# Loads by heads, one engine per q/k copy, MoE steps in the order of w_in, a third PSUM bank, batch 1 three slots later

## The chip, the cores and the metric

One core of one Trainium2 chip. The metric is the device time of one execution in microseconds (us); the kernel before takes 350.98 us, the median of four runs from 350.35 to 351.89. Engines are called by the profile's names: PE (TensorE matmul; PEld its weight loads), DVE (VectorE), ACT (ScalarE), POOL (GpSimd), SP (SyncE). POOL also issues the loads from HBM.

## The reference

A sliding-window attention with ALiBi bias is followed, without a return to HBM, by a two-layer feed-forward with ELU (called MoE in the code, though there is one expert). Inputs are float32; the kernel computes in float16 with float32 sums.

```
q, k, v: (8 batches, 8 heads, 576 positions, 64)
scores = q k^T / 8;  key within the last 128 positions: scores - slope_h * distance, else -1e9
attn = softmax(scores);  x = (attn v) as (4608 tokens, 512)
h = x w_in          (512 x 2048)
g = where(h > 0, h, exp(min(h, 0)) - 1)
out = g w_out       (2048 x 512)
```

## The kernel before

**Attention.** 576 positions are five key/query blocks: four of 128, stored interleaved, and a tail of 64. One step of attention is one entry of `BANKS`, a block and two or four heads, so that its scores fill one PSUM bank of 512 columns; a batch has 16 steps. A step has `scores` (PE, L355; for batch 0 the bias is added by PE too, L375, for the other batches by extra rows of q and k), an exponential on ACT (L379, 512 columns), for batches 1 to 7 a minimum with a mask, `cut`, on DVE (L387), and `values` (PE, L401). When both head halves of a block are there, `normalize` divides on DVE (L421, L422), and `turn` transposes the result into `xT`, in batches 0 and 1 by PE through a PSUM bank and a DVE copy (L435, L437), later by DMA. q and k must stand with the head dimension on partitions: for batch 0 `transposes_half`, for batch 1 `transposes`, both by PE and copied out of PSUM by `put` (L305), which gives one half of the columns to DVE and the other, after it, to ACT. From batch 2 on DVE's `squares` (L324) and DMAs do it.

**Values.** v is loaded in another layout, and 32-partition pieces of it are copied into the buffers `VP`, by DVE (L119) or by POOL (`place_by_pool`, L124, two pieces to a call). Sixteen pieces make a batch. POOL does twelve pieces of batches 0 and 1 each and all of the rest.

**MoE.** A block of 512 tokens takes 16 first-layer steps and 16 second-layer steps. A first-layer step, `hidden`, is 16 (or 8 wider) matmuls into one PSUM bank `hp` (L458), an exponential on ACT (L462) and a clamp on POOL (L463); `elu` on DVE (L470) joins the two in the next slot and frees the bank. There are two such banks, so that a step must wait for the `elu` two steps earlier. A second-layer step, `output`, is four matmuls of 512 columns into the one bank `op` (L501); each fourth is followed by an ACT copy (L505), which frees that bank, and by the stores. Matmul step m of the first layer uses the columns of w_in, and of the second the rows of w_out, in four chunks that POOL loads one by one.

**The order.** It is written out by hand. The last loop runs over slots: in each it emits `hidden`, the `elu` of the slot before, the tasks entered for the slot by `at`, and `output`. `HID` and `OUT` say which step falls into which slot, `LATER` pushes them back from some step on. Each engine executes its instructions in this order and waits where an operand isn't there. A DMA that POOL issues uses one of eight completion semaphores in turn, so that the ninth issue waits for the first one's landing. `warm` (L533) issues matmuls whose result nobody reads.

```
for m in range(16 * NTB):
    late = LATER.get(m, late)
    HID[4 + m + late[0]] = OUT[13 + m + late[1]] = divmod(m, 16)
for b in range(B):
    s0 = 16 * b                        # scores of step s in slot s0 + s
```

In the kernel before, batch 0 takes slots 0 to 15, batch 1 slots 16 to 31 and so on; the first layer starts in slot 4, the second in slot 13, and the last output step is in slot 160. A slot of the steady part (one first-layer step, one second-layer step, one attention step) is some 2.1 us long.

Of the kernel before, what the change touches and what calls it, by code (L numbers as in the profile page):

```python
# [12 lines left out]
ALU = mybir.AluOpType  # L13
# [6 lines left out]
def kernel(  # L20
# [20 lines left out]
    LATER = {16: (0, 1), 24: (1, 2), 30: (2, 2), 32: (3, 3), 40: (4, 4)}  # L41
# [9 lines left out]
    ps_x = ctx.enter_context(tc.tile_pool(name="ps_x", bufs=1, space=PSUM))  # L51
    ps_h = ctx.enter_context(tc.tile_pool(name="ps_h", bufs=2, space=PSUM))
# [34 lines left out]
    def load_half(b, w, a):  # L87
        if b not in stq:
            stq[b] = stage.tile([128, 2, H, 4, D], F16, name="stq")
        nc.gpsimd.dma_start(  # L90
            stq[b][64 * a:64 * a + 64, w, :, :, :].rearrange("p h j d -> p h (j d)"),
            (q, k)[w][b, :, 256 * a:256 * a + 256, :].rearrange("h (p j) d -> p h (j d)", j=4))
# [24 lines left out]
    def place_v4(b, n):  # L117
        for j in range(4):
            V.tensor_copy(VP[b % 2][32 * j:32 * j + 32, n, :, 0:D],  # L119
                          vs[b][32 * n:32 * n + 32, :, j, :])  # L120

    def place_by_pool(b, n, u):
        for j in (2 * u, 2 * u + 1):
            nc.gpsimd.tensor_scalar(  # L124
                out=VP[b % 2][32 * j:32 * j + 32, n, :, 0:D], in0=vs[b][32 * n:32 * n + 32, :, j, :],
                scalar1=1.0, scalar2=0.0, op0=ALU.mult, op1=ALU.add)
# [12 lines left out]
    with tc.manual_schedule():  # L139
# [3 lines left out]
        posi = one([128, 576], I32, "posi")  # L143
        nc.gpsimd.iota(row, pattern=[[0, 1]], base=0, channel_multiplier=1)
        nc.gpsimd.iota(col, pattern=[[1, 128]], base=0, channel_multiplier=0)
        load_half(0, 1, 0)
        load_half(0, 0, 0)
# [8 lines left out]
        load_v_half(0, 1)  # L156
        load_wi(2)
        load_wi(3)
# [73 lines left out]

        def terms():

            nc.gpsimd.tensor_scalar(out=is96, in0=rowf, scalar1=96.0, scalar2=None, op0=ALU.is_equal)
            nc.gpsimd.tensor_scalar(out=is97, in0=rowf, scalar1=97.0, scalar2=None, op0=ALU.is_equal)
            nc.gpsimd.tensor_scalar(out=isx, in0=is97, scalar1=-1.0, scalar2=None, op0=ALU.mult)
            nc.gpsimd.tensor_scalar(out=pm[r_, :], in0=posi[r_, :], scalar1=float(-MID), scalar2=None,
                            op0=ALU.add)
            nc.gpsimd.tensor_scalar(out=TQ[r_, 0:576], in0=pm[r_, :], scalar1=isx[r_, :], scalar2=is96[r_, :],  # L240
                            op0=ALU.mult, op1=ALU.add)
            nc.gpsimd.tensor_scalar(out=TK[r_, 0:576], in0=pm[r_, :], scalar1=is96[r_, :],
# [4 lines left out]
        def group_rows():  # L247
# [5 lines left out]
            for t in (TQ, TK):  # L253
                V.tensor_copy(t[g_, 256:512], t[g_, 0:256])

# [16 lines left out]
        zeros()  # L272
        groups()

# [6 lines left out]
        def transposes_half(a, hq):  # L281

            if a:
                t = ps_o.tile([128, 2, 2, 4, 2, 32], F16, name="tph", tag="op")
            else:
                t = ps_s.tile([128, 2, 2, 4, 2, 32], F16, name="tp", tag="sps")
            p = slice(64 * a, 64 * a + 64)
            for w in (1, 0):
                for g in range(4):
                    for j in range(2):  # L290
                        nc.tensor.transpose(
                            t[:, w, :, g, j, :],
                            stq[0][p, w, 4 * hq + g, 2 * j:2 * j + 2, :].rearrange("p a d -> p (a d)"),
                            ident[p, p])
            for n in range(2):
                put(t[:, :, n], QK[0][0:64, 2 * a + n, :, 4 * hq:4 * hq + 4, :])
# [371 lines left out]
```

## Time and profile before

| | |
|---|---|
| median of 4 runs | 350.98 us (350.35 to 351.89) |
| profiled execution, its own time | 350.35 us |
| span of its records | 348.6 us |
| PE busy | 329.1 us (94%) |
| DVE busy | 247.9 us (71%) |
| POOL busy | 222.0 us (64%) |
| ACT busy | 189.5 us (54%) |
| matmuls that nobody reads (L533) | 90, 9.6 us |
| HBM read, written | 36.70 MB, 9.44 MB |

Busy time is the union of the records of an engine; a matmul's record overlaps the next one's, so that start to start is the better measure for PE (four output matmuls show 1.03 us as one piece, and the next instruction starts 0.86 us after their start). A row of the timeline gives the start, the length, the engine, the line and operation, the tiles, and in brackets how long the engine was idle before and what ended that.

### The profile page before, as it was taken

To read this page: it belongs to the slowest core of one execution; us is meant where nothing else is said; L and a number is where in the kernel's file an instruction comes from. 1 tells how busy PE (TensorE), PEld (TensorE's weight loads), DVE (VectorE), ACT (ScalarE), POOL (GpSimd) and SP (SyncE) were. 2 spreads that over 40 slices of the span, in tenths; PEclk is the share of its full clock that TensorE was granted. 3 is DMA by queue.
4 is the path that set the end of the run, shared out by engine and by line. 5 is a ranking of instruction groups with operands and counts; after the bars stand their busy time and mean duration, and the time that the engine had idled before them with its cause. 6 is when DMAs were issued, how large, how long until landed. Compare 5 with 4: busy or idle time off the path is not lost.

```text
span 348.6 us, 9340 instructions
## 1 busy us (share of the span) xinstructions
PE 329.1 (94%) x3610; PEld 242.8 (70%) x3610; DVE 247.9 (71%) x556; ACT 189.5 (54%) x335; POOL 222.0 (64%) x344
## 2 busy tenths in 40 slices
PE   6998799877999999999999999999999999999995
PEld 5876677655676677777777777777777777666653
DVE  5664797587689789978987889789977666433330
ACT  4457675654556565555565565555555665444431
POOL 9698858999748965894688488748832223333320
PEclk9699999999999999999999999999999999999999
DMA  8999997259994599469956974895432222121122
GB/s 105 197 207 202 138 152 102 40 100 181 182 146 100 115 176 130 100 118 185 135 116 104 200 109 109 127 187 97 107 75 57 55 54 47 40 59 31 30 50 73
DMA packets 66075, 39.53 MB, mean 113 GB/s; under 512 B 31024, under 2 KB 59952, under 8 KB 65968
## 3 DMA queue, kind: packets, MB, share of 16 engines
q0 software_dynamic: 41904, 18.35, 44.7%
q1 hardware_dynamic: 23952, 20.46, 27.0%
q8 instruction: 28, 0.46, 0.5%
q10 hardware_dynamic: 176, 0.13, 0.1%
q14 instruction: 15, 0.12, 0.1%
HBM read 36.70 MB, written 9.44 MB: 132 GB/s over the span
## 4 chain that ended last, share of the span: by engine, by line
PE 69%; POOL 13%; DVE 5%; DMA 5%; issue 4%; ACT 2%; SPq 1%; POOLq 0%; ACTq 0%; DVEq 0%
PE hp L458 30%; PE op L501 28%; POOL VP L124 6%; PE sp L355 6%; PE av L401 4%; POOL e L463 3%; DMA wi<-in_moe_w_in_dram 2%; DVE g L470 2%; DMA stt<-in_q_dram 1%; DVE tt L324 1%; SPq L507 1%; DVE xn L422 1%; DVE EX L387 1%; ACT EX L379 1%; POOL stq L83 1%
## 5 line engine op out<-in xcount | busy, mean ns | idle before, releaser
L458 PE MATMUL hp<-xT,wi 128*128 128x256 f16 (+3 forms) x1536 | 150.4, 246 | 8.0 <-DVE g L470 5.2
L458 PEld LDWEIGHTS <-wi 128*128 128x128 f16 x1536 | 120.6, 98 | 49.6 <-DVE g L470 10.2
L463 POOL TENSOR_SCALAR e<-e 128x512 f32<-128x512 f32 x144 | 89.9, 624 | 100.3 <-ACT e L462 92.4
L462 ACT ACTIVATE e<-hp 128x512 f32<-128x512 f32 x144 | 86.0, 597 | 120.4 <-PE hp L458 113.6
L501 PE MATMUL op<-wo,g 128*128 128x512 f16 x560 | 143.0, 379 | 0.0
L470 DVE SCALAR_TENSOR_TENSOR g<-e,hp 128x512 f16<-128x512 f32 x144 | 96.9, 673 | 45.8 <-POOL e L463 45.4
L124 POOL TENSOR_SCALAR VP<-vs 32x512 f16<-32x512 f16 x120 | 76.4, 637 | 10.0 <-DMA vs<-in_v_dram 1.8
L379 ACT ACTIVATE EX<-sp 128x512 f16<-128x512 f32 x128 | 75.9, 593 | 11.7 <-PE sp L375 7.9
L387 DVE TENSOR_TENSOR EX<-EX,band 128x512 f16<-128x512 f16 x112 | 56.9, 508 | 27.3 <-ACT EX L379 26.5
L501 PEld LDWEIGHTS <-g 128*128 128x128 f16 x560 | 49.6, 98 | 35.0
L355 PE MATMUL sp<-QK 128*128 128x128 f16 (+3 forms) x576 | 50.1, 214 | 0.8 <-ACT QK L305 0.8
L401 PE MATMUL av<-VP,EX 128*128 128x65 f16 x576 | 38.8, 194 | 1.8 <-DVE EX L387 1.8
L401 PEld LDWEIGHTS <-EX 128*128 128x128 f16 x576 | 32.4, 98 | 5.4 <-DVE EX L387 2.8
L422 DVE TENSOR_TENSOR xn<-av,rden 128x256 f16<-128x256 f32 x80 | 34.0, 425 | 2.7
L324 DVE STREAM_TRANSPOSE tt<-stq 128x512 f16<-128x512 f16 x48 | 33.1, 697 | 0.0
L355 PEld LDWEIGHTS <-QK 128*128 128x128 f16 (+1 forms) x576 | 31.5, 97 | 2.0 <-ACT QK L305 1.2
L505 ACT COPY ob<-op 128x512 f32<-128x512 f32 x35 | 20.5, 586 | 10.3 <-PE op L501 5.2
L421 DVE RECIPROCAL rden<-av 128x4 f32<-128x4 f32 x80 | 13.9, 174 | 3.8 <-PE av L401 3.4
L533 PE MATMUL spare<-ident 128*128 128x128 f16 x90 | 9.6, 288 | 1.6 <-DVE ident L165 1.6
L305 ACT COPY QK<-tp 64x512 f16<-64x512 f16 (+1 forms) x8 | 6.3, 795 | 7.9 <-DVE QK L305 7.9
L533 PEld LDWEIGHTS <-ident 128*128 128x128 f16 x90 | 8.4, 135 | 1.8 <-DVE ident L165 1.6
L343 DVE COPY QK<-tpt 64x512 f16<-64x512 f16 x16 | 6.7, 417 | 0.3 <-PE tpt L338 0.2
(75 smaller groups left out, 134.0 us busy)
## 6 DMA issues: line engine op xcount, KB each, us to landing
out_dram<-ob SPq DMA_DIRECT2D x126, 64.0 KB, 1.9
QK<-tt SPq DMA_DIRECT2D x48, 128.0 KB, 2.3
stq<-in_k_dram POOLq DMA_DIRECT2D x7, 512.0 KB, 8.2
stq<-in_q_dram POOLq DMA_DIRECT2D x7, 512.0 KB, 8.5
vs<-in_v_dram POOLq DMA_DIRECT2D x7, 512.0 KB, 11.3
wi<-in_moe_w_in_dram POOLq DMA_DIRECT2D x4, 512.0 KB, 11.7
wo<-in_moe_w_out_dram POOLq DMA_DIRECT2D x4, 512.0 KB, 13.5
QK<-QK SPq DMA_DIRECT2D x1, 1280.0 KB, 8.6
```

The source lines that it names most:

```text
L124: nc.gpsimd.tensor_scalar(out=VP[b % 2][32 * j:32 * j + 32, n, :, 0:D], in0=vs[b][32 * n:32 * n + 32, :, j, :], scalar1=1.0, scalar2=0.0, ...
L324: V.transpose(out=tt[b][:, dh, w, hs, :, :].rearrange("p h j i -> p (h j) i"), in_=stq[b][:, w, hs, :, 32 * dh:32 * dh + 32].rearrange("p ...
L355: nc.tensor.matmul(t[:, o:o + n], qk[0:r, kc, 1, h, :], qk[0:r, qc, 0, h, 0:n], start=b > 0 or o == 0, stop=b > 0)
L379: nc.scalar.activation(e[:, 0:512], t, AF.Exp, scale=0.125)
L387: V.tensor_tensor(out=e, in0=e, in1=band[:, c:c + n].unsqueeze(1).broadcast_to([128, 512 // n, n]), op=ALU.min)
L401: nc.tensor.matmul(a[:, l, :], e[:, c:c + 128], vp[:, n, h, 0:D + 1], start=st, stop=sp)
L422: V.tensor_tensor(out=xnt[b, i][:, 4 * half:4 * half + 4, :], in0=a[:, :, 0:D], in1=r.unsqueeze(2).broadcast_to([128, 4, D]), op=ALU.mult)
L458: nc.tensor.matmul(p[:, l * w + u0:l * w + u1], w_in_sb[:, c, fc * 128:(fc + 1) * 128], xT[:, c, x0:x0 + u1 - u0], start=(c == 0), stop=(c ...
L462: nc.scalar.activation(e, p, AF.Exp)
L463: nc.gpsimd.tensor_scalar(out=e, in0=e, scalar1=1.0, scalar2=0.0, op0=ALU.min, op1=ALU.max)
L470: V.scalar_tensor_tensor(out=gs[t][:, f0:f0 + nf, c0:c0 + w], in0=sh(es.pop((t, j))), scalar=1.0, in1=sh(hps.pop((t, j))), op0=ALU.subtrac ...
L501: nc.tensor.matmul(ops[t], gs[t][:, fc, ts * 128:(ts + 1) * 128], w_out_sb[:, fc, :], start=(fc == 0), stop=(fc == NFC - 1))
```

## The change

- The first halves of k and q of batch 0 are loaded in two groups of four heads. The first group's DMAs now stand ahead of the two index generators (`iota`) from which the identity matrix is made.
- `transposes_half` treats one of q and k at a time, in a bank of its own; ACT copies k, DVE copies q, in four pieces of 256 columns each. The banks come from other pools than before.
- `place_v` replaces `place_v4` and `place_by_pool` and takes the engine. In batch 0's first two blocks ACT, DVE and POOL share the pieces; in batches 1 and 2 POOL and ACT take one piece each where POOL took two.
- The terms of the bias rows are made on DVE, in slots 3 to 10, where POOL made most of them in slot 0. Loads of w_in (chunks 2, 3), of w_out and of the second half of v are issued by POOL between its pieces, in slots 0 to 10.
- The first eight first-layer steps come in the order 0, 1, 4, 5, 2, 6, 3, 7 (those that use chunks 0 and 1 of w_in before those that use 2 and 3), and from step 2 on two slots later. The bank for the transposes of `turn` is given up (they use those of the scores), and `hp` gets it as its third.
- Batch 0's steps 6 to 15 come 2 slots later, all other batches 5 slots later; first-layer steps from 16 on move by 5 slots in all, second-layer steps by 3. The last output step is in slot 163. There are 68 unread matmuls instead of 90.

```diff
-    LATER = {16: (0, 1), 24: (1, 2), 30: (2, 2), 32: (3, 3), 40: (4, 4)}
+    LATER = {16: (3, 4), 24: (4, 5), 30: (5, 5), 32: (6, 6), 40: (7, 7)}
-    ps_x = ctx.enter_context(tc.tile_pool(name="ps_x", bufs=1, space=PSUM))
-    ps_h = ctx.enter_context(tc.tile_pool(name="ps_h", bufs=2, space=PSUM))
+    ps_h = ctx.enter_context(tc.tile_pool(name="ps_h", bufs=3, space=PSUM))
...
+    def place_v(b, n, js, engine):
+        for j in js:
+            o, i = VP[b % 2][32 * j:32 * j + 32, n, :, 0:D], vs[b][32 * n:32 * n + 32, :, j, :]
+            if engine is nc.gpsimd:
+                engine.tensor_scalar(out=o, in0=i, scalar1=1.0, scalar2=0.0, op0=ALU.mult, op1=ALU.add)
+            elif engine is V:
+                engine.tensor_copy(o, i)
+            else:
+                engine.copy(o, i)
...
+        load_half(0, 1, 0, 0, 4)
+        load_half(0, 0, 0, 0, 4)
         nc.gpsimd.iota(row, pattern=[[0, 1]], base=0, channel_multiplier=1)
         nc.gpsimd.iota(col, pattern=[[1, 128]], base=0, channel_multiplier=0)
-        load_half(0, 1, 0)
-        load_half(0, 0, 0)
+        load_half(0, 1, 0, 4, 8)
+        load_half(0, 0, 0, 4, 8)
...
-        def transposes_half(a, hq):
+        def transposes_half(a, hq, w, pool, tag):
...
             for n in range(2):
-                put(t[:, :, n], QK[0][0:64, 2 * a + n, :, 4 * hq:4 * hq + 4, :])
+                for odd in range(2):
+                    (nc.scalar.copy if w else V.tensor_copy)(
+                        QK[0][0:64, 2 * a + n, w, 4 * hq:4 * hq + 4, :].rearrange(
+                            "p h (a o i) -> p h a o i", o=2, i=32)[:, :, :, odd, :],
+                        t[64 * odd:64 * odd + 64, n])
...
+        first = [0, 1, 4, 5, 2, 6, 3, 7]
         for m in range(16 * NTB):
             late = LATER.get(m, late)
-            HID[4 + m + late[0]] = OUT[13 + m + late[1]] = divmod(m, 16)
-        warm(34)
-        transposes_half(0, 0)
+            t, j = divmod(m, 16)
+            HID[m + (4 if m < 2 else 6) + late[0]] = t, first[m] if m < 8 else j
+            OUT[13 + m + late[1]] = t, j
+        warm(20)
+        transposes_half(0, 0, 1, ps_h, "hp")
         warm(8)
+        transposes_half(0, 0, 0, ps_h, "hp")
+        transposes_half(0, 1, 1, ps_v, "av")
         at(0, scores, 0, 0)
-        at(0, transposes_half, 0, 1)
-        at(0, warm, 12)
-        at(0, place_v4, 0, 0)
+        at(0, transposes_half, 0, 1, 0, ps_v, "av")
+        at(0, warm, 8)
+        at(0, place_v, 0, 0, (0, 1), V)
+        at(0, place_v, 0, 0, (2,), nc.scalar)
+        at(0, place_v, 0, 0, (3,), nc.gpsimd)
+        at(0, place_v, 0, 1, (0, 1, 2), nc.gpsimd)
+        at(0, load_v_half, 0, 1)
+        at(0, load_wi, 2)
...
         for b in range(B):
-            s0 = 16 * b
+            s0 = 16 * b + (5 if b else 2)
...
+                sv = s if b == 0 and s < 6 else s0 + s
...
-                    at((13, 14, 15, 15)[hp], transposes, 1, hp)
+                    at((18, 19, 20, 20)[hp], transposes, 1, hp)
                 for n in range(8 if b else 0):
-                    at(s0 + (2 + n if b > 1 else 6 + n // 2), squares, b + 1, n)
+                    at(s0 + (2 + n if b > 1 else 4 + n), squares, b + 1, n)
...
+        at(8, terms)
+        at(3, zeros)
+        at(8, last_blocks)
+        at(5, groups)
+        at(10, group_rows)
+        at(20, place_v, 1, 0, (0, 1, 2, 3), V)
         for n in range(4):
             for u in range(2):
                 if n:
-                    at(13 + 2 * n + u, place_by_pool, 1, n, u)
-                at(21 + 2 * n + u, place_by_pool, 2, n, u)
+                    at(18 + 2 * n + u, place_v, 1, n, (2 * u,), nc.gpsimd)
+                    at(18 + 2 * n + u, place_v, 1, n, (2 * u + 1,), nc.scalar)
+                at(26 + 2 * n + u, place_v, 2, n, (2 * u,), nc.gpsimd)
+                at(26 + 2 * n + u, place_v, 2, n, (2 * u + 1,), nc.scalar)
```

## The prediction

> **What bounds the kernel now.** I read the busy shares first, then the waits of PE, then stretches of the span.
>
> ```profile
> PE 329.1 (94%) x3610; PEld 242.8 (70%) x3610; DVE 247.9 (71%) x556; ACT 189.5 (54%) x335; POOL 222.0 (64%) x344
> ```
>
> PE is the bound, and its work hardly changes. What can move is its idle time, 19.5 of 348.6 us, and the unread matmuls. The table of stretches (length; busy us and count for PE, PEld, DVE, ACT, POOL; granted clock; DMA) says where it idles:
>
> ```profile
> 1.60:6.10 4.50, 4.41 (x42) 3.99 (x42) 2.56 (x13) 2.13 (x9) 4.50 (x8) 1.00 0.89 114
> 6.10:9.50 3.40, 1.68 (x24) 1.28 (x25) 2.22 (x11) 0.93 (x2) 3.40 (x6) 1.00 1.24 159
> 9.50:16.40 6.90, 6.61 (x69) 5.84 (x69) 4.71 (x13) 2.60 (x5) 4.21 (x8) 0.51 1.33 199
> ...
> 18.70:51.20 32.50, 28.36 (x435) 23.42 (x433) 22.42 (x54) 22.02 (x34) 26.53 (x39) 1.00 1.23 173
> 51.20:57.80 6.60, 6.60 (x93) 5.22 (x92) 5.56 (x16) 4.87 (x9) 4.45 (x7) 1.00 0.74 89
> 57.80:90.70 32.90, 26.93 (x350) 19.26 (x349) 21.95 (x48) 18.08 (x30) 29.98 (x44) 1.00 0.66 112
> 90.70:200.00 109.30, 108.24 (x1219) 79.45 (x1219) 92.62 (x206) 62.35 (x114) 77.87 (x120) 1.00 0.94 139
> ```
>
> After 90.7 us PE idles 1 us in 109; nothing is to be won there. It idles 4.1 us in 18.7 to 51.2 (slots 4 to 15) and 6.0 us in 57.8 to 90.7 (slots 19 to 30), where POOL is busy 91% of the time. Note the third row: after a stretch in which PE was busy 1.68 of 3.4 us the granted clock was half for 6.9 us. The timelines of PE and POOL inside the last idle stretch show the mechanism:
>
> ```profile
> 75.12 1.55 POOL L124 TENSOR_SCALAR VP<-vs 32x512 f16<-32x512 f16 x2
> 76.76 0.61 POOL L463 TENSOR_SCALAR e<-e 128x512 f32<-128x512 f32 x1
> 77.32 0.72 POOL L104 DMA_DIRECT2D stt<-in_k_dram  x1
> 78.10 1.57 POOL L124 TENSOR_SCALAR VP<-vs 32x512 f16<-32x512 f16 x2
> ...
> 78.15 1.05 PE L458 MATMUL hp<-xT,wi 128*128 128x128 f16 x16 [0.73 <-DVE g L470]
> ```
>
> The clamp (L463) stands behind two v pieces and a load in POOL's queue, `elu` waits for it, and with two banks the first layer waits for `elu`.
>
> **The change, stretch by stretch.** I walk through the new order with the durations of these records and the waits that the order implies. Sums are against the profiled execution (span 348.6, own time 350.35); the median of the runs is 0.63 above that, and I add differences to the median.
>
> *Start to the first first-layer matmul (18.69 before).* The identity waits for two load issues more (first k load 0.87 and first q load 0.69 for eight heads; taken as 0.6 each for four), so `warm` begins at 2.97, not 1.62. Twenty unread matmuls at the first ones' 112 ns end at 5.2, where the landed k is transposed (5.48 before; earlier landing alone would be hidden behind the identity). Separate engines then copy q and k at once: four pieces of 0.29 on DVE (a 256-column DVE copy of PSUM shows 0.29) beside four of 0.37 on ACT (256 columns: 0.37), 1.5 us instead of 0.42 + 0.58 + 0.42 + 0.58 in turn. First score at 8.5 (8.73), second at 11.1 (12.12), then the slots with 16 unread matmuls less: first MoE matmul at 17.0. **-1.7.** Bounds: 0 (the later identity eats it) and -2.7 (all 22 dropped matmuls at 122 ns).
>
> *Slots 4 to 20, before 4 to 15.* PE's share of a slot, start to start: first-layer step 0.89, score and value with batch 0's bias 0.8, output step 0.86, eight transposes 0.44. Slots 6 and 7 hold no first-layer step: values, 32 transposes and a turn, 1.7 us of work, but 3.6 us long, since scores, exponential, copies and normalisation follow each other (0.65 + 0.35 + 0.75 + 0.15 idle). Slots 8 and 10 pile on DVE: bias terms (two of about 0.5, a row that DVE doesn't have; a 256-column one takes 0.34, POOL's 1.02; bounds 0.35 and 1.0) and the last blocks' mask, 3.3 together, then the group rows, 1.9. DVE's sum over slots 8 to 13 is 11.4 against PE's 11.1, begins 1.0 behind, and delays `elu`: PE waits 0.95, 0.5 and 0.4, though the third bank shifts each wait one slot back. POOL has 10.1 us here and w_in, w_out land in time (chunk 2 issued near 13.5, needed near 28). Length 38.3 against 32.5, with three first-layer steps and five output steps more done (3 x 0.89 + 5 x 0.86 = 7.0): **-1.2.** Bounds -3 and +1.5 (DVE pieces 20% longer beside POOL, as one v piece's 0.74 beside a 0.28 minimum shows is possible).
>
> *Slots 20 to 24, before 15 to 18.* Here the change adds a wait. In slot 20 ACT's queue is: exponential 0.6, two halves of transposed q/k (a pair shows 1.92, DVE's 0.68 ahead of it), a v piece, then the copy that frees `op`. A v piece on ACT has no row; 128 columns from SBUF take 0.29 beginning to end (0.21 in sequence), 1024 take 1.04, so 512 lie between 0.3 and 1.04, by interpolation 0.61. Already late from slot 18 (bias rows 1.04), the copy starts 4.8 and ends 5.4 us into slot 20, whereas the next output step is ready at 3.7. PE waits 1.7 us, and behind that wait stand the exponential of batch 1's first scores and its cut, so that the values wait 0.85 more, then 0.45. Slots 22 to 24 have no first-layer step to fill in, as the next needs batch 1's first block. Slots 21 to 23 take 7.6 us with one first-layer step; before, slots 16 to 18 took 6.66 with three: 7.6 + 2 x 0.89 - 6.66 = **+2.7.** Bounds 0 (v piece at 0.3, and the copy just in time) and +3.2.
>
> *Slots 24 to 35, before 19 to 30.* POOL's sum falls from 27 to 18 us, one v piece a slot having gone to ACT. But slots 29 to 32 have no output step (before: only slot 29), while DVE has elu 0.69, cut 0.45, a square 0.70 and half a normalisation in each of slots 25 to 32: 19.9 us in slots 25 to 33 against 16.2 of PE. The bound goes from POOL to DVE: PE waits for the cut 0.7, 1.35, 0.85, 1.8 in slots 30 to 33. By the walk 28.1 us, before 32.9 with one first-layer step and three output steps more (3.5): **-1.25.** Bounds -5 (DVE's lag bridged) and +1.
>
> *Rest:* the same slots, shifted; two output steps fewer trail at the end, but the sum of PE's work is the same: 0. Sum -1.45.
>
> *The clock.* The wait in slots 21 and 22 leaves PE 0.86 us of work in some 3.4 us, less than the 1.68 of 3.4 after which the clock was half for 6.9 us. [...] Then 6.9 us at half clock cost 3.4 us of PE work, of which 0.7 fall into waits that slots 22 to 25 have anyway: +2.7. I go by the row. Sum **+1.25**, 350.98 + 1.25 = 352.2.
>
> **The rivals.** (1) *As walked, full clock:* 349.5. [...] (2) *Not slower: TensorE runs ahead of DVE.* The third bank lets the first layer go on while the cuts are late, and slots 24 to 35 shrink to PE's own 22.6 us plus what DVE can't bridge, -5 instead of -1.25; with it, 352.2 - 3.75 = 348.5, and 345.8 at full clock. It decides once PE's idle time in these slots is under 3 us where I have 5.2. For it: from 98 to 108 us before, DVE ended up to 2.4 us behind PE's slot without stopping PE. Against: that was with values two slots after scores; batch 1 has one. (3) *Worse on both counts:* slots 6 and 7 (1.7 of 3.6 us busy) also bring half a clock, +1.9 after DVE's waits there, and DVE is stretched by ACT's and POOL's copies, +1.5: 355.6. (4) *Loads by heads do nothing:* the first score waits for the identity and copies, the start gains 0: 353.9, part of (3)'s side.
>
> **How the numbers follow.** The main case has 0.35 (own range 351 to 353.8), (1) 0.23, (2) 0.2, (3) and (4) 0.22. A measurement of this kernel can tell about 0.3%, 1.05 us, from no change. Below 349.93 lie (2) and most of (1): 0.38. Within 1.05 us lie the edges of (1) and of the main case: 0.12. Above: 0.5. The range leaves a tenth on each side: low 345.8, case (2) at full clock; high 357, (3) with the start's bound of +1.7 nearly whole.
>
> **What the profile would show.** Start: first L458 record near 17 us. Slot 20: an idle PE ahead of an output matmul near 59 us, ended by the ACT copy of `op`, about 1.7 us, and half the granted clock after it. Then PE waits for the DVE cut, 1 us and more each, near 75 to 85 us, with POOL under 80% busy. It would be wrong if ACT reaches the `op` copy in time, if PE's idle time between 18 and 95 us is below 8 us in all, or if the clock is full there.

## The result and the profile after

The changed kernel takes 349.28 us (median of 43 runs, 347.22 to 352.61), the kernel before 350.74 (64 runs): ratio 0.9957, 95% interval 0.9944 to 0.9969; the ratios here leave out slow runs, over 1.5% above the fastest of their kernel (the 352.61 is one). It is faster by 0.4%, 1.5 us; I had forecast 1.25 us slower. The profiled execution took 348.65 us (before: 350.35), with a span of 346.9 us.

The busy shares of the changed kernel, first. Its `elu` is on L468, the first layer on L456, the scores on L353, the copy of the output bank on L503.

```profile
PE 329.2 (95%) x3588; PEld 244.3 (70%) x3588; DVE 248.8 (72%) x568; ACT 200.8 (58%) x359; POOL 211.1 (61%) x326
```

PE's sum is that of before; 11 us left POOL and 11 us came to ACT. Then the stretches that answer to those shown of before (length; busy us and count for PE, PEld, DVE, ACT, POOL; granted clock; DMA): the start, slots 4 to 20, slots 21 to 23, slots 24 to 35, one step of half clock in these, and the rest.

```profile
6.80:9.50 2.70, 2.44 (x30) 1.94 (x28) 1.38 (x5) 2.20 (x7) 1.92 (x3) 1.00 1.11 138
...
20.00:55.78 35.78, 33.64 (x473) 26.24 (x471) 29.48 (x74) 24.18 (x41) 26.83 (x40) 1.00 1.21 166
55.78:63.22 7.44, 4.91 (x49) 2.87 (x48) 5.56 (x13) 6.26 (x10) 5.08 (x8) 1.00 1.09 150
63.22:91.81 28.59, 24.62 (x321) 18.61 (x320) 21.61 (x47) 22.33 (x37) 18.75 (x29) 0.94 0.62 105
84.70:88.20 3.50, 3.50 (x27) 2.44 (x25) 1.58 (x5) 1.21 (x2) 0.78 (x2) 0.51 0.67 136
91.81:200.00 108.19, 107.41 (x1219) 80.45 (x1218) 88.81 (x203) 63.07 (x114) 78.38 (x118) 1.00 0.95 139
```

The third row is where I had put the half clock. PE is busy 4.91 of 7.44 us there, and the clock is full. Slots 24 to 35 (fourth row) lost POOL as their bound: 18.75 of 28.59 us busy, before 29.98 of 32.90. PE idles 4.0 us in them instead of 6.0; between 18 and 95 us it idles 8.6 us in all, just above the 8 us that I had named as a sign of being wrong. A half clock does occur, but in the fifth row, after DVE's late cuts. (The clock record of this profile begins at 16.45 us; the 1.00 that the first row shows is not a record. The same 128-column matmuls show 314 ns up to 16.4 us and 219 ns after it, as they do before and after 16.37 us in the kernel before, where the record has the clock at half from 9.54 to 16.37 us; so the clock was half here too.)

The wait for the output bank that I had walked through (1.7 us) is there to a tenth. The timeline of PE, slots 20 to 22:

```profile
58.73 1.02 PE L499 MATMUL op<-wo,g 128*128 128x512 f16 x4 [1.67 <-ACT ob L503]
60.26 0.30 PE L399 MATMUL av<-VP,EX 128*128 128x65 f16 x4 [0.52 <-DVE EX L385]
```

The waits of PE over the whole changed kernel hold a line that no part of the prediction speaks of, the last here:

```profile
PE av L399 <- DVE EX L385: 4.3, 8, 1.3
...
PE op L499 <- ACT ob L503: 1.7, 1, 1.7
...
PE hp L456 <- DVE g L468: 0.5, 1, 0.5
...
PE sp L353 <- DMA QK<-tt: 0.3, 1, 0.3
```

It is the first score of batch 2 (slot 37), which waits for q and k of batch 2 as `collect` copies them over SP's queue. It looks small. It became the second finding of the study.

### The profile page after: what moved, and what is told of

Its sections match the earlier page's. It is cut to its first block, busy times and chain, and to the rows that moved or that the text cites. A ratio compares the mean times of both kernels' runs of the same rounds, so it can differ in the third digit from the quotient of the medians.

```text
span 346.9 us, 9316 instructions
## 1 busy us (share of the span) xinstructions
PE 329.2 (95%) x3588; PEld 244.3 (70%) x3588; DVE 248.8 (72%) x568; ACT 200.8 (58%) x359; POOL 211.1 (61%) x326
## 4 chain that ended last, share of the span: by engine, by line
PE 67%; DVE 5%; DMA 3%; ACT 2%; SPq 1%; issue 1%; DVEq 0%; ACTq 0%
PE op L499 29%; PE hp L456 29%; PE sp L353 6%; PE av L399 4%; DMA QK<-tt 2%; DVE g L468 2%; DVE tt L322 1%; DVE EX L385 1%; ACT EX L377 1%; DMA xT<-xn 1%; SPq L328 1%; ACT e L460 1%; DVE xn L420 0%; PE tpt L336 0%; SPq L505 0%
## 5 line engine op out<-in xcount | busy, mean ns | idle before, releaser
L456 PE MATMUL hp<-xT,wi 128*128 128x256 f16 (+3 forms) x1536 | 151.1, 247 | 1.1 <-DMA xT<-xn 0.5
L456 PEld LDWEIGHTS <-wi 128*128 128x128 f16 x1536 | 123.0, 98 | 39.6 <-issue 2.6
L468 DVE SCALAR_TENSOR_TENSOR g<-e,hp 128x512 f16<-128x512 f32 x144 | 96.8, 672 | 38.7 <-POOL e L461 38.0
L385 DVE TENSOR_TENSOR EX<-EX,band 128x512 f16<-128x512 f16 x112 | 54.7, 488 | 30.2 <-ACT EX L377 29.8
L121 POOL TENSOR_SCALAR VP<-vs 32x512 f16<-32x512 f16 x106 | 68.4, 645 | 12.9 <-DMA vs<-in_v_dram 5.6
L353 PE MATMUL sp<-QK 128*128 128x128 f16 (+3 forms) x576 | 50.2, 215 | 0.5 <-DMA QK<-tt 0.3
L353 PEld LDWEIGHTS <-QK 128*128 128x128 f16 (+1 forms) x576 | 31.7, 98 | 1.7 <-issue 0.6
L503 ACT COPY ob<-op 128x512 f32<-128x512 f32 x35 | 20.5, 586 | 10.0 <-PE op L499 7.6
L531 PE MATMUL spare<-ident 128*128 128x128 f16 x68 | 8.2, 301 | 3.8 <-DVE kmod L169 3.8
L125 ACT COPY VP<-vs 32x512 f16<-32x512 f16 x16 | 9.8, 615 | 0.8 <-DMA vs<-in_v_dram 0.4
L531 PEld LDWEIGHTS <-ident 128*128 128x128 f16 x68 | 6.8, 141 | 4.1 <-DVE kmod L169 3.8
L373 PE MATMUL sp<-DM,cI 128*128 128x256 f16 (+1 forms) x40 | 6.9, 279 | 0.0
```

The costliest lines, as they stand in the source:

```text
L121: engine.tensor_scalar(out=o, in0=i, scalar1=1.0, scalar2=0.0, op0=ALU.mult, op1=ALU.add)
L353: nc.tensor.matmul(t[:, o:o + n], qk[0:r, kc, 1, h, :], qk[0:r, qc, 0, h, 0:n], start=b > 0 or o == 0, stop=b > 0)
L385: V.tensor_tensor(out=e, in0=e, in1=band[:, c:c + n].unsqueeze(1).broadcast_to([128, 512 // n, n]), op=ALU.min)
L456: nc.tensor.matmul(p[:, l * w + u0:l * w + u1], w_in_sb[:, c, fc * 128:(fc + 1) * 128], xT[:, c, x0:x0 + u1 - u0], start=(c == 0), stop=(c ...
L468: V.scalar_tensor_tensor(out=gs[t][:, f0:f0 + nf, c0:c0 + w], in0=sh(es.pop((t, j))), scalar=1.0, in1=sh(hps.pop((t, j))), op0=ALU.subtrac ...
```

## The experiments

My theory for the miss: the walk without the half clock was right (349.5), and the clock depends on something finer than a half-busy 3.4 us. The rivals: the third bank did more than I gave it; the start gained more; or what was lost and won before 95 us didn't reach the end. All times are medians; each ratio is to runs of the kernel before on the same chip (350.5 to 350.7 us), with its 95% interval. The changed kernel's own ratio is 0.9957.

### The pieces on ACT, and the wait in slot 20

One edit gives only the pieces of slots 20 and 21 back to POOL:

```
-  at(18 + 2 * n + u, place_v, 1, n, (2 * u + 1,), nc.scalar)
+  at(18 + 2 * n + u, place_v, 1, n, (2 * u + 1,), nc.gpsimd if n == 1 else nc.scalar)
```

> The changed kernel, with the two v pieces of slots 20 and 21 given back from ACT to POOL. If the wait for the output bank in slot 20 (1.7 us in the changed kernel) comes from the v piece and what stands with it in ACT's queue: the piece is 0.62 us of the 1.7, so about 1.1 us of wait is left and the waits behind it shrink too, 348.3 us. If that wait only hides a later one (the values of slot 21, which wait for the cut): no change, 349.3. If POOL is late instead (values of batch 1 wait for v): 350 or more.

Measured: 348.35 us, ratio 0.9918 (0.9896 to 0.9940). The wait for the bank fell from 1.67 to 1.02 us, by the 0.6 of one piece, and the time by what was expected. (By the limit estimated below from a count of columns, the shorter wait also leaves no position of the clock's steps that would bring a half clock there: no stretch of one step's length in this profile's slots 20 to 24 holds fewer than 3,440 columns.)

A second gives all pieces of batches 1 and 2 back:

```
-  at(18 + 2 * n + u, place_v, 1, n, (2 * u + 1,), nc.scalar)
+  at(18 + 2 * n + u, place_v, 1, n, (2 * u + 1,), nc.gpsimd)
-  at(26 + 2 * n + u, place_v, 2, n, (2 * u + 1,), nc.scalar)
+  at(26 + 2 * n + u, place_v, 2, n, (2 * u + 1,), nc.gpsimd)
```

> The changed kernel, with all v pieces of batches 1 and 2 on POOL, none on ACT, as in the kernel before (13 pieces of some 0.75 us more on POOL in slots 20 to 33). Theory of my walk: POOL's sum there rises from 18 to about 28 us and the clamp stands behind the pieces again, so what the change won in slots 24 to 35 (1.25 us) is lost, and about 0.7 is won back in slot 20, where the output bank waits for ACT: 349.8. Rival: the third bank bridges POOL's queue by itself, and the move to ACT only costs the wait in slot 20: 348.3.

Measured: 350.03 us, ratio 0.9971 (0.9947 to 0.9994). By the ratios that is 0.5 us above the changed kernel, with overlapping intervals: what all the pieces on ACT are worth together is not proved by this run. But it is 1.9 us above the kernel with only two pieces given back, and these two intervals don't overlap: the pieces of slots 22 and later are worth having on ACT, those of slots 20 and 21 are not. The wait for the bank is 1.0 here too; the waits for the cut grew from 4.3 to 5.6, the longest, 2.3 us, at 85.2 us. (PE also waits 1.5 us for `elu` instead of 0.5, but at 30 to 33 us, ahead of the edit's first slot; that is not its doing.)

A third puts two more on ACT, which write again what another copy writes:

```
+  at(20, place_v, 1, 1, (3,), nc.scalar)
+  at(20, place_v, 1, 2, (1,), nc.scalar)
```

> The changed kernel with two further v pieces on ACT in slot 20 (they write again what another copy writes), so that the wait for the output bank there grows by 1.2 us, from 1.7 to 2.9. Rule that ten profiles suggest: in steps of 3.41 us, whose beginning differs from execution to execution, PE's columns are counted (those of a 64-row matmul half), and fewer than some 3,000 to 3,100 give half the clock for the next step. With the longer wait most positions of the steps have fewer (with 1.7 us a quarter of them): a half clock near 57 to 64 us in the profile, and 1.2 us for the wait plus most of 1.7 for the clock, less what is absorbed at the scores of batch 2 (0.3 to 1.3): 350.5 to 352. Rival, a step must be empty of matmuls: no half clock at 55 to 65 us, 349.5 to 350.5.

Measured: 350.18 us, ratio 0.9986 (0.9966 to 1.0005). The wait is 2.9 us, as the sum of two pieces has it, so the queue on ACT is shown as the cause of the wait. On the clock this run says nothing for the theory: the time lies in the rival's range, and in the profile the clock stayed full there, with 3,384 columns in the step around the wait (the count is explained below). By the limit estimated there 88% of the positions of the steps would have given a half clock, so either this execution was one of the few others or the limit does not hold for it; the other eleven executions have no profile.

### The third bank

The changed kernel with two banks, and the kernel before with three:

```
-    ps_h = ctx.enter_context(tc.tile_pool(name="ps_h", bufs=3, space=PSUM))
+    ps_x = ctx.enter_context(tc.tile_pool(name="ps_x", bufs=1, space=PSUM))
+    ps_h = ctx.enter_context(tc.tile_pool(name="ps_h", bufs=2, space=PSUM))
-            t = ps_s.tile([128, 4, 128], F16, name="xps", tag="sps")
+            t = ps_x.tile([128, 4, 128], F16, name="xps", tag="xps")
```

> The changed kernel with two banks for the first layer, and the bank of its own for the transposed x, as before. My walk gave the third bank only a shift of the waits in slots 8 to 13 by one slot, and left slots 24 to 35 to DVE: 0.3 to 0.9 us longer, 349.6 to 350.2. Rival 2 of the prediction (the bank lets TensorE run ahead of a late DVE and POOL): 2 to 4 us of waits of the first layer for elu come back in slots 8 to 13 and 24 to 35, 351.5 to 353.

Measured: 350.79 us, ratio 0.9998 (0.9976 to 1.0021): by the medians all of the gain is gone without the bank. PE's waits, with two banks:

```profile
PE hp L457 <- DVE g L469: 4.8, 7, 1.4
PE av L400 <- DVE EX L386: 2.9, 5, 1.3
PE op L500 <- ACT ob L504: 1.7, 1, 1.7
PE hp L457 <- DMA xT<-xn: 1.3, 1, 1.3
```

The first layer waits 4.8 us for `elu` where it waited 0.5. Part of that is taken from the wait for the cut (2.9, was 4.3). By the medians the bank is worth 1.5 us (from 0.5 to 2.4 by the intervals of the two ratios together), more than the 0.3 to 0.9 of my walk, less than rival 2 needed. Part of it lies where neither my walk nor rival 2 looked, behind slot 37: the kernel before waits once more for `elu` there, at 143.0 us, the changed kernel does not, and with two banks it waits twice, at 122.9 and 141.3 us. PE's waits between 133 and 147 us before, then between 110 and 150 us with two banks:

```profile
PE hp L458 <- DVE g L470: 0.7, 1, 0.7
```

```profile
PE hp L457 <- DVE g L469: 1.1, 2, 0.6
```

> The kernel before with the third bank alone (the transposed x goes into the scores' banks). If POOL's queue sets the pace of slots 19 to 30 (busy 91%), a bank more only shifts the waits there: 350.0 to 350.7. If the bank bridges what POOL is late by, part of the 6.0 us of idle time there goes: 347.5 to 349, and the bank would be what made the changed kernel faster.

Measured: 350.00 us, ratio 0.9986 (0.9961 to 1.0010): not told from no change. In the kernel before, the bank moves the waits from the first layer (0.3 us is left there) to the cut (4.0) and to x's transposes (1.9), which now share the scores' banks. Its profile also had a half clock from 38.3 to 45.2 us. By this run the bank alone is not shown to pay; with the rest of the change it is.

### Squares of batch 2 earlier

```
-    at(s0 + (2 + n if b > 1 else 4 + n), squares, b + 1, n)
+    at(s0 + (2 + n if b > 1 else 1 + n), squares, b + 1, n)
```

> The changed kernel, with the eight squares of batch 2 in slots 22 to 29 instead of 25 to 32. Theory: DVE is the bound in slots 29 to 33, so three squares of 0.70 us fewer there take 2 of the 3.2 us that PE waits in slots 29 to 33, and with it the half clock after them; the squares in slots 22 to 24 lie in time in which DVE waits for ACT's late queue anyway: 346.5 to 347.5. Rival: the squares delay the cuts of slots 22 to 24 by 0.7 each, what is won later is lost there: 349 to 350.

Measured: 349.78 us, ratio 0.9991 (0.9972 to 1.0011). A miss. The half clock near 85 us was absent in its profile (mean granted clock 0.998), but what was won by slot 33 came out again as waits for transfers: 1.6 us for a load of q's tail at 88.8 us, 1.1 us at the first score of batch 2, the line noticed above, and 1.1 instead of 0.5 us for the DMA-transposed x. (The 1.4 us of waits for `elu` in this profile lie at 28 to 33 us, ahead of the edit.)

### The clock: filling a wait

The changed kernel, with unread matmuls ahead of the values of slots 31 and 32:

```
+    FILL = {9: 6, 10: 20}
...
+    if b == 1 and s in FILL:
+        for _ in range(FILL[s]):
+            nc.tensor.matmul(a[:, 2 * (p % 2), :], ident, ident[:, 0:D + 1], start=True, stop=True)
```

> The changed kernel, with 26 unread matmuls of 65 columns ahead of the values of slots 31 and 32, where PE waits 0.3 and 1.3 us for DVE's cut; they write a region that the values then write anew. Theory: the half clock from 84.72 to 88.13 us comes from a stretch of 3.41 us with too few columns in it (1.41 us of PE's busy time); with 1,300 columns more in it the clock stays full, which is worth half of 3.41 us, 1.7 us, in the executions that have that stretch: 347.6 to 348.5, and no half clock near 85 us in the profile. Rival, the clock does not go by what PE does there: half clock as before, 349.3 to 349.8.

Measured: 351.26 us, ratio 1.0020 (0.9999 to 1.0040). The clock behaved as the theory said, full from 64 to 347 us. The time did not, and is some 2 us above the changed kernel's: the first score of batch 2 waited 1.3 us for its transfers instead of 0.3 and came at 95.7 us, as in the changed kernel (95.8), and the DMA-transposed x was waited for 1.9 us instead of 0.5. That second wait, which the other kernel with fillers below has too (1.8), is not explained. Nor do the executions without a profile show the fuller clock: the twelve have a mean granted clock of 0.992, as those of the changed kernel have, though a half step fewer adds 0.005. The surprise was elsewhere: this profile had a half clock at 60.68 us, in slots 21 to 23, where my prediction had put it and where the edit changes nothing.

### Where the clock's steps fall

Every change of clock in these profiles lies on a grid of 3.41 us whose beginning differs from execution to execution (6.13, 9.54 and 16.37 us in the first profile of the kernel before, 16.45, 84.72 and 88.13 in that of the changed kernel). For each step I counted the columns that PE streamed: a 512-column matmul takes 0.216 us at full clock (four begin 0.86 us before the next group), so each was spread over that rate, and a matmul with 64 rows was counted half. At this rate a step at full clock holds some 8,090 columns; the fullest on record count 8,050 to 8,100. In the 18 profiles:

```
columns in a step of 3.41 us, full clock granted   -> clock in the next step
20 steps with 1,590 to 3,127                       -> half
all others: lowest 2,977  3,076  3,076  3,087      -> full
at half clock: 2,560 2,652 2,687 2,698 2,808       -> stays half
               3,317 and more                      -> full
```

A limit near 3,050, some 38% of a full step, is my estimate from these counts; it separates both directions, with two of some 1,740 steps on its wrong side. The edges of the count are uncertain by about 100, and by more at half clock. Steps just ahead of a profile's first clock record, taken at half clock, had 3,090 and more and were followed by full clock. The half weight of 64-row matmuls is a choice of this count: counting each transpose by PE half and every other matmul whole separates the steps as well, in each direction by itself. What the clock itself goes by is not shown. By the estimated limit, a quarter of all positions of the grid give the changed kernel a half clock after slot 21, if the matmuls stand where its first profile has them. Only further executions of the unchanged kernels can test that.

> The changed kernel, unchanged, profiled once more: the profile of an execution tells where the clock's steps of 3.41 us fall in it, and that differs from execution to execution. By the rule of the column count (below some 3,050 full-row columns in a step: half clock in the next), a clock record that begins at 57.4 us or up to 0.9 us ahead of it, less whole steps, has the half clock after slots 21 and 22 that step 5 of the prediction foresaw (a quarter of executions); the others don't. The start: full clock from about 7 us in some, from about 16.4 in others, the first MoE matmul at some 15 or some 17.4 us. If the rule is wrong, the clock is as in the first profile, or changes without regard to the steps.

Measured: 347.13 us. In this execution of the changed kernel a step begins at 54.71 us. The stretches of one step each:

```profile
54.71:58.12 3.41, 1.24 (x9) 0.39 (x7) 2.40 (x6) 3.32 (x6) 1.38 (x3) 1.00 1.10 142
58.12:61.53 3.41, 3.41 (x22) 1.99 (x23) 2.03 (x6) 1.42 (x3) 3.15 (x5) 0.50 1.01 139
61.53:64.94 3.41, 3.29 (x42) 2.29 (x41) 1.46 (x3) 3.30 (x6) 1.39 (x3) 1.00 0.02 5
```

The wait fills most of the first (2,157 columns), and the next is at half clock: the clock that the prediction foresaw, in the changed kernel itself. The same wait in the first profile of the changed kernel, by its own grid, and the steps around the late cuts:

```profile
57.41:60.82 3.41, 1.58 (x13) 0.75 (x13) 2.41 (x7) 2.82 (x6) 1.44 (x3) 1.00 1.26 176
60.82:64.24 3.42, 2.50 (x22) 1.23 (x21) 2.52 (x7) 2.81 (x4) 3.17 (x5) 1.00 0.78 98
81.31:84.72 3.41, 1.40 (x22) 0.90 (x20) 3.38 (x8) 2.30 (x4) 2.73 (x5) 1.00 1.52 306
84.72:88.13 3.41, 3.41 (x25) 2.35 (x23) 1.56 (x5) 1.21 (x2) 0.76 (x2) 0.50 0.66 134
```

The wait is cut by the grid: 3,295 columns in the first step, and the clock stays full. In the third, 1,998 columns, and it is halved.

> The changed kernel, unchanged, a second such look: as for the first, and own time and clock go together: with full clock from about 7 us some 1.5 to 2.5 us shorter than with full clock from 16.4 us, and a half stretch in slots 6 and 7, 21 and 22, or 31 and 32 costing up to 1.7 us each, less what the scores of batch 2 wait for their transfers in any case.

Measured: 347.53 us; half clock at 82.57 us, after a step of 2,209 columns; full clock at slots 21 to 23 (3,544).

> The changed kernel, unchanged, a third such look: as for the first two. By the rival view (only a step without any matmul halves the clock) no execution has a half clock between 16.5 and 84 us.

Measured: 348.83 us; half clock at 23.65 us, around slots 6 and 7 (1,755 columns in the step before), and at 85.09 (2,834). No step in the three was empty of matmuls, and each has a half clock between 16.5 and 84 us (58.12, 82.57, 23.65): the rival view does not hold here.

> The kernel before, unchanged, profiled once more. By the column count its only stretches with few columns lie at the start and around 37 us (3,076 in one step of the first profile, at the edge): the half clock of the start (6.9 us in the first profile) depends on where the steps fall as well, and so does the first MoE matmul (18.69 us): between 16.5 and 19 us.

Measured: 349.84 us; half clock from 8.77 to 15.60 us, first MoE matmul at 18.67. The kernel before does the same as in its first profile.

Side by side, all from the clock records and PE's timeline (us):

```
execution          own time  full clock from  first MoE matmul  later half steps  wait of slot 37
changed, first      348.65       16.45            17.43          84.72              0.26
changed, 2nd        347.13        6.92            14.86          58.12              1.67
changed, 3rd        347.53        7.47            15.17          82.57              1.24
changed, 4th        348.83       13.41            16.28          23.65, 85.09       0.22
before, first       350.35     6.13 to 9.54, 16.37   18.69       none               none
before, 2nd         349.84     5.36 to 8.77, 15.60   18.67       none               none
```

Two things follow. In the four executions of the changed kernel the position of the grid goes with how long its start takes: the earlier the full clock, the earlier the first MoE matmul, by up to 2.6 us. And the execution with the half clock that the prediction foresaw is the fastest of the four. What that half clock cost can be read against the 3rd for a while: the sixteenth `elu` ends at 58.60 and 58.55 us, the nineteenth at 73.19 and 72.23. It cost 0.9 us by then. Behind that the pair tells nothing, since the 3rd had its own half step at 82.57 us. At slot 37 PE's lead shrinks in any case: at the twenty-fifth `elu` the four stand 2.9 us apart (90.45, 87.52, 88.11, 90.22), at the twenty-eighth 1.6 (97.96, 96.40, 96.68, 97.92), the early ones having waited longest there.

It would be wrong to conclude that half clocks cost nothing in the end. Each of the 44 executions of the changed kernel on record has its mean granted clock, from which one half step takes 0.005. The 23 with 0.992 or more have a median of 348.8 us, the 21 with 0.990 or less one of 350.0. Where their half steps fell is known for the profiled ones alone.

### Behind slot 37: a transfer that was moved

The diff moves `fill_other`, one transfer of 64 rows of 20 KB, from slot 24 to slot 30, by 6. Batch 1, with the `collect` transfers of batch 2 that share its queue (slots 24 to 31, now 29 to 36), moves by 5 slots (three more than batch 0). What changed is what stands behind it. Before, it was issued at 75.1 us, the next collect at 82.8, and it landed at 83.7. In the changed kernel it is issued at 79.8 us, the next collect 0.7 us behind it, and it lands after 8.9 us, at 88.7; that collect lands at 89.1. The collects of the changed kernel (79 to 97 us), issues and time to landing:

```profile
L328 SPq DMA_DIRECT2D QK<-tt x8: 520/636/2613, 78.5 to 89.0; - x8
...
DMA to landing us min/median/max: 2.4/9.0/10.8
```

Before, seven collects were issued after 80 us:

```profile
L330 SPq DMA_DIRECT2D QK<-tt x7: 513/540/591, 82.8 to 91.3; - x7
...
DMA to landing us min/median/max: 3.1/3.5/7.0
```

The median landing rose from 3.5 to 9.0 us. One edit puts the transfer ahead again:

```
-        at(30, fill_other)
+        at(27, fill_other)
```

> The changed kernel with the copy of batch 1's bias rows to the other q/k buffer (64 rows of 20 KB, one transfer) in slot 27 instead of 30. Theory, from four traces in which TensorE comes to the scores of batch 2 at times 3.4 us apart in slot 33 and at the same time, 95.6 to 95.8 us, in slot 37: the collected q/k of batch 2, whose transfers stand behind this copy, set the time there and absorb what is won or lost in slots 21 to 36. With the copy ahead of them the first ones land 3 us earlier; in executions with no half clock in slots 21 to 36 PE then gains 1 to 2 us, in the others 0.3: 348.3 to 349. Rival: the loads of batch 3's q and k, which start at the same time, hold the collected rows back just as long: 349.3.

Measured: 347.12 us (6 runs), ratio 0.9897 (0.9866 to 0.9929), 0.6% below the changed kernel and more than expected. The collects with it:

```profile
L328 SPq DMA_DIRECT2D QK<-tt x8: 508/580/1342, 79.6 to 86.7; - x8
...
DMA to landing us min/median/max: 2.8/5.6/7.3
```

The wait of slot 37 is gone from PE's waits. This profile alone would not show much, since PE comes as late in it as in the first one (twenty-fifth `elu` at 90.35 and 90.45 us), where the wait was 0.3; the combined kernel below comes at 86.80 and doesn't wait there either. The rival, that batch 3's loads would hold the rows back anyway, falls for the first four collects, which land in 2.8 to 4.3 us; the last four, issued behind the first of these loads (84.0 us), still take 7.0 to 7.3. Other kernels that come early, the one with the pieces of slots 20 and 21 on POOL and the two with the iotas first below, wait 1.8, 1.1 and 1.1 us for a load of q's tail instead, at 90 us; issued beside `fill_other`, this load landed after 9.3 us in the first profile, and after 4.7 with the transfer moved.

### The start

The iotas ahead of the loads, with 34 unread matmuls first instead of 20:

```
-        load_half(0, 1, 0, 0, 4)
-        load_half(0, 0, 0, 0, 4)
         nc.gpsimd.iota(row, pattern=[[0, 1]], base=0, channel_multiplier=1)
         nc.gpsimd.iota(col, pattern=[[1, 128]], base=0, channel_multiplier=0)
+        load_half(0, 1, 0, 0, 4)
+        load_half(0, 0, 0, 0, 4)
         load_half(0, 1, 0, 4, 8)
         load_half(0, 0, 0, 4, 8)
...
-        warm(20)
+        warm(34)
```

> The changed kernel, with the two iotas ahead of all four loads by heads, and 34 unread matmuls first instead of 20, as before. By my step on the start, the identity then is ready 2.2 us earlier, the first transposes no longer wait for it and come at 5.5 instead of 6.0 us, first MoE matmul 0.5 us earlier; with a full clock from about 6 us on, which the kernel before had for one stretch and the changed one had not at all before 16.45 us, another 0.5: 348.3. If the loads, issued 0.3 us later, set the first scores: no change, 349.3.

Measured: 347.92 us, ratio 0.9928 (0.9905 to 0.9951). First score at 7.92 us, first MoE matmul at 14.27, full clock from 6.74. Its interval and the changed kernel's just overlap; the direction is as expected.

The same with each load for eight heads:

```
-        load_half(0, 1, 0, 0, 4)
-        load_half(0, 0, 0, 0, 4)
-        load_half(0, 1, 0, 4, 8)
-        load_half(0, 0, 0, 4, 8)
+        load_half(0, 1, 0)
+        load_half(0, 0, 0)
```

> The changed kernel with the iotas ahead of the loads and 34 unread matmuls, as in the run with the iotas first (347.9 us), but each of q and k of batch 0 loaded for eight heads at once: the loads by heads alone. By my step on the start, q's first half lands 1.4 us later (6.9 instead of 5.5), and the first scores come 0.8 us later: 348.7. By rival 4 of the prediction, the first scores wait for the identity and the copies: 347.9.

Measured: 347.86 us, ratio 0.9926 (0.9906 to 0.9946): the same. PE waits 0.6 us for q in its profile, and the first score comes at 8.23 instead of 7.92 us, but nothing of this is left at the end. The loads by heads alone are worth nothing that these runs can tell. (Its profile, with a step from 55.97 us and 2,279 columns, is the third with a half clock after slot 21, of ten whose wait in slot 20 is 1.7 us; by the estimated limit it would be a quarter.)

### Together

The edits shown above for the pieces of slots 20 and 21 (on POOL), for `fill_other` (slot 27) and for the iotas (first, with 34 unread matmuls), in one kernel:

> Three edits together: the v pieces of slots 20 and 21 back to POOL, the iotas first with 34 unread matmuls, and the copy of bias rows in slot 27. Alone they gave 0.9, 1.4 and 2.2 us against the changed kernel. If the copy of bias rows let the others' gain through at the scores of batch 2, they add up: 345 to 346. If the transfers of batch 2 and 3 from 95 to 110 us are a second bound: 347.

Measured: 345.42 us (6 runs), ratio 0.9867 (0.9836 to 0.9898). This version beats both kernels, by 1.3% and 0.9%. PE's waits in it, with none for a transfer at slot 37:

```profile
PE av L399 <- DVE EX L385: 4.9, 8, 1.3
...
PE op L499 <- ACT ob L503: 1.0, 1, 1.0
PE top L285 <- ACT QK L291: 0.8, 1, 0.8
```

The same with fillers in slots 6, 31 and 32:

```
+    FILL = {(0, 5): 16, (1, 9): 6, (1, 10): 20}
...
+    if (b, s) in FILL:
```

> The same three edits, with 42 unread matmuls of 65 columns in PE's waits of slots 6, 31 and 32. Alone, in slots 31 and 32, they kept the clock full there, and the time was no shorter, since the scores of batch 2 waited for their transfers. If that was the reason, they are worth up to 1.7 us in the executions with a half clock there now, 0.5 to 1 in the median against the kernel with the three edits alone: 344.5 to 345.5. If they cost more than they give: 346 or more.

Measured: 345.93 us (4 runs), ratio 0.9874 (0.9856 to 0.9891): no gain. Its profile has no half clock at slots 31 and 32, but neither has that of the version without fillers; the step ahead of 22.18 us held 2,237 columns in spite of the fillers in slot 6, and the wait for the DMA-transposed x was 1.8 us again.

## Why the prediction was wrong

*The failed step is the clock (+2.7).* It said that the wait in slots 21 and 22 leaves 0.86 us of PE's work in some 3.4 us and that half clock for 6.9 us follows. Three of its parts were off. It took the worst position of a 3.4-us stretch as the one that occurs; the grid began elsewhere in each of the six executions of the table, and by the estimated limit about a quarter of its positions give the half clock (one of four profiles of the changed kernel, three of ten with those of its variants that have the same wait). It took the length, 6.9 us, from a row at the start, where the second step too held too few columns (2,687); here the step after the wait is full of output matmuls (4,120 columns) and the clock is back after 3.41 us. And it put the cost at 2.7 us where the one that occurred cost 0.9 us by the nineteenth `elu`; how much of that reached the end no run shows. A quarter of 0.9 us, by an estimate from these two figures, would have been the term. Without the step the sum was -1.45, 349.5 us; measured, -1.46 and 349.28.

The row that I went by, half a step busy, was right on the amount, since the halved steps held 1,590 to 3,127 columns where a full one holds some 8,090, and silent on the position: in the four profiles of the changed kernel the grid began at four different times. No run shows a cost of 2.7 us.

*Start (-1.7).* Sign right, size too small and its reason in part wrong. 17.0 us was forecast; four profiles show 17.43, 14.86, 15.17 and 16.28 against 18.67 and 18.69 before, -1.2 to -3.8. The identity was later than walked: the first unread matmul came at 3.8 us, not 2.97. The first score did not come earlier for certain (8.36 to 8.83, before 8.72 and 8.73), and the loads by heads are worth nothing alone, which is rival 4's mechanism without its price. What is left are the unread matmuls taken out, and the full clock that now comes from 7 or 8 us on in some executions (two of the four profiles, six of the eleven with this start). I had priced everything up to 16.4 us at the half clock of one profile.

*Slots 4 to 20 (-1.2).* Right: slot 21 begins 38.35 us after the first MoE matmul, 38.3 forecast. Single waits were smaller (0.5 us for `elu` where 0.95, 0.5 and 0.4 were walked), which the bank bridged: with two banks they are 0.7 and 1.4 us.

*Slots 20 to 24 (+2.7).* Right: 1.67 us of wait for the bank (1.7), then 0.52 and 0.34 (0.85, 0.45); slots 21 to 23 took 7.44 us (7.6). The v piece took 615 ns on ACT (0.61). Taking one piece away and adding two moved the wait by 0.65 and 1.27.

*Slots 24 to 35 (-1.25).* Right in kind: 28.59 us (28.1), the bound gone from POOL to DVE, waits for the cut of 0.88 and 1.34. Within them lies a half clock that the walk had not foreseen, after DVE's waits; three of the four profiles have it.

*Rest (0).* Wrong, and the second failure, in two ways. I passed over `fill_other`: with the collects now close behind it, it puts 1.3 MB in front of them on SP's queue. The scores of batch 2 then wait 0.2 to 1.7 us, the more the earlier PE comes. That the transfer costs about 2 us (0.9 to 3.3 by the intervals of the two ratios together) is shown by moving it; how they are shared among executions is not. And I gave the third bank nothing behind slot 37: from the twenty-eighth `elu` to the 139th the four executions of the changed kernel take 231.1 to 231.3 us, the two of the kernel before 231.8 and 232.1, most of it the wait for `elu` at 143 us.

So the agreement of -1.45 with -1.46 is partly luck. In the first profile of each kernel, with the work moved between stretches counted as in the prediction, the terms come to -1.3 (start), -1.1, +2.6, -0.8 and, for the rest, -1.1: the errors of the start, of slots 24 to 35 and of the rest cancel. In the early executions the start won more, and the wait of slot 37 took part of it back.

*Rivals.* The first (as walked, full clock, 349.5) is what came. Rival 2's mechanism was real at a smaller size: the bank is worth 1.5 us by the medians, but slots 24 to 35 did not shrink to PE's work (4.0 us of idle time where under 3 would have decided for it). Rival 3's clock in slots 6 and 7 occurs too, in one of four profiles, without the rest of its loss.

## What to carry to other kernels

In these traces a half clock was an event with a chance, not a fixed cost: after slot 21 it came in one of four profiles of the changed kernel. To price one, I would look for the stretches where TensorE streams under some 38% of what a 3.41-us step holds (my estimate from the counts of these traces), ask how many positions of the grid put a whole step into them, and multiply by what the next waits don't absorb. When a schedule is shifted, list every transfer with its old and new place relative to the work that it serves; one that now stands close ahead of others on its queue is where a gain can end (here in 0.2 to 1.7 us of wait at slot 37). Time won ahead of such a wait shows in no total, so compare two executions at several points along the span before you trust a sum that fits.

## What the runs showed of the hardware that was not expected

- In the 18 profiles the changes of the clock lie on a grid of 3.41 us, and its beginning differed between executions of the same kernel (full clock from 6.92, 7.47, 13.41 and 16.45 us). With 64-row matmuls counted half, 20 steps at full clock with 1,590 to 3,127 columns were followed by half clock, all others, with 2,977 and more, by full; steps at half clock with 2,560 to 2,808 were followed by half, those with 3,317 and more by full. The half weight is what made the steps with transposes and scores of 64 rows fit: one with 3,712 columns by number, 2,688 by rows, was followed by half clock. Half weight for the transposes alone fits as well, so which of the two describes the clock stays open.
- The same kernel's first MoE matmul moved between 14.86 and 17.43 us from execution to execution, in the order in which the full clock began (6.92 to 16.45 us).
- One 64-row, 20-KB-a-row transfer ahead of 4-KB-a-row ones on the same queue raised their median time to landing from 3.5 to 9.0 us, beside batch 3's loads; with the transfer three slots earlier it was 5.6.
